# One 4 MB weight load in two halves on two queues, and two 1 KB loads moved to GpSimd

## The chip, the cores and the metric

The kernel runs on one core of a Trainium2 chip. Its time is device microseconds (us) of one execution, and what is compared is the median of several executions. A profile is one further execution, recorded instruction by instruction; its times are counted from the start of its span.

## What is computed

The kernel is one decode step of a block that mixes two branches by a gate. With one token `x` of 512 numbers:

```python
g = sigmoid((x * gate_w).sum(-1))
q = x @ wq                        # 512 x 4096: 32 heads of 128
k, v = the last 4096 rows of 8 cached heads, each shared by 4 query heads
a = softmax(q k^T / sqrt(128)) v @ wo
b = (sigmoid(x @ w_gate) * (x @ w_up)) @ w_down
out = g * a + (1 - g) * b
```

All inputs are bf16. What has to be read is 30.67 MB: `wq` and `wo` 4 MB each, the keys and the values 8 MB each, and `w_gate`, `w_up`, `w_down` 1.75 MB each. The result is 1 KB. Every weight is used once, for one row.

## The kernel before, in words

**Loads.** All large loads are issued by SyncE (SP) on one queue, in the order written in the kernel: `wq` (line 80, one DMA of 128 partitions x 32 KB), four key blocks `kn` of 2 MB (line 84, in a helper called four times), `w_gate` (94), most of `w_up` (99), the rest of `w_up` as four loads `wx` of 32 partitions (105), four value blocks `vv` (84 again), two halves of `wo` (115), and `w_down` in four pieces `wd` (120). The two 1 KB inputs `x` and `gate_w` are issued by ScalarE (ACT) on its own queue (lines 74 and 75). They land in the one-partition tile `xr`. The result leaves by ScalarE's queue too (343).

**Waits of the loads.** The framework deals the loads that SyncE and ScalarE issue over eight semaphores in turn, so a load may be issued only when the load eight places before it has landed. A `vv` load also waits until the transposes on VectorE (DVE) have read the `kn` buffer that it overwrites, and `wo` waits for the last reader of `wq_sb`.

**Start of the compute.** GpSimd (POOL) builds an identity (`identf`, `ident`), a block of ones, a zeroed `qbig` and a permutation (lines 123 to 133). TensorE (PE) turns `x` into a column `xT` by four tiny matmuls against `ident` (148), and a piece of it into `xx` (155) after VectorE has copied it to `xp` (153). VectorE multiplies `x` by `gate_w` and sums (165, 166), makes `selI` and `other` (143, 140), and copies `xT` and `xx` out of PSUM (158, 160). VectorE takes its work in exactly this order, so everything from line 165 on stands behind the landing of `gate_w`. TensorE then fills the score banks with a mask (182, it needs `other`), sums the gate (168), and starts on `q`.

**The rest.** `q` is 8 blocks of 4 matmuls (200) that need `xT` and `wq_sb`; ScalarE copies each block out (202), VectorE transposes (205) and scatters into `qbig` (216). Eight key transposes on VectorE (188) feed 64 score matmuls (227). Softmax, then 64 value matmuls (299) as the value blocks arrive, then the up projection (243, 240), `wo` and `w_down` row by row into one accumulator (290), and two copies to `res` (341, 342). The order on TensorE, VectorE and ScalarE is that of the program text from line 177 on.

Of the kernel before, what the change touches and what calls it, by code (L numbers as in the profile page):

```python
# [17 lines left out]
def kernel(  # L18
# [14 lines left out]
    nc = tc.nc  # L33

    P = 128
# [35 lines left out]


    xr = const.tile([1, 2, D], BF16, name="xr")
    nc.scalar.dma_start(xr[:, 0, :], A_x[0, :, :])
    nc.scalar.dma_start(xr[:, 1, :], gate_w.rearrange("(o n) -> o n", o=1))

    dq = nc.sync
    wq_sb = big.tile([P, DC, HQ * DH], BF16, name="wq_sb", tag="big")
    wq_v = A_wq.rearrange("(p c) n -> p c n", c=DC)
    dq.dma_start(wq_sb[:], wq_v)  # L80


    def load_pair(t, cache, a, n0=0, n1=NP):
# [290 lines left out]
```

## Time and profile before

| | us |
|---|---|
| median of 6 executions | 80.45 (80.27 to 80.68) |
| the profiled execution's own time | 80.68 |
| its span in the profile | 79.0 |
| TensorE busy | 52.4 |
| VectorE busy | 38.8 |
| ScalarE busy | 10.9 |
| GpSimd busy | 3.3 |
| DMA bytes / mean rate over the span | 30.71 MB / 389 GB/s |

The span leaves out 1.7 us of the profiled execution's own time (80.68 less 79.0), which lie before its first and after its last instruction. The profile names 16 DMA engines; its queue q1 carries SyncE's loads (2608 packets, 30.67 MB, 92.4% of the 16 engines' span), and q10 carries ScalarE's (6 packets). A "packet" is what one engine moves at a time: for `wq` a whole row of 32 KB. The trace also keeps when each engine reported the end of its share of a load ("landing"). In the timeline a suffix q (SPq, ACTq) is the sequencer of an engine issuing a DMA.

### The profile page before, as it was taken

How to read it: one execution, taken by the hardware profiler on the slowest of the kernel's cores; microseconds unless marked ns; L12 is line 12 of the kernel's file. 1: busy time of each engine (PE TensorE's matmuls, PEld its weight loads, DVE VectorE, ACT ScalarE, POOL GpSimd, SP SyncE). 2: the span in 40 equal slices, each digit the busy share in tenths (PEclk: the TensorE clock that was granted, in tenths of full speed). 3: DMA queues.
4: the chain of work that ended last, by engine and by line, in shares of the span. 5: the costliest groups of instructions: out<-in, count | busy, mean ns of one | idle time of the engine just before them, and what ended most of it. 6: DMA issues, size and time to landing. Idle time of an engine off the chain costs nothing.

```text
span 79.0 us, 798 instructions
## 1 busy us (share of the span) xinstructions
PE 52.4 (66%) x314; PEld 23.6 (30%) x314; DVE 38.8 (49%) x52; ACT 10.9 (14%) x20; POOL 3.3 (4%) x10
## 2 busy tenths in 40 slices
PE   0200182999914788998888307999996699567650
PEld 0200131344402333333332202344341345345420
DVE  1601820019959999999996339963000000690020
ACT  2400000237742000000001191000000002000010
POOL 7900000000000000000000000000000000000000
PEclk9999999999999999999999995699999999999997
DMA  6779899999999999999999999999999999999700
GB/s 183 282 332 515 381 431 390 415 440 448 423 415 464 423 415 414 436 414 428 405 466 390 423 440 440 423 415 440 431 440 398 423 440 448 398 398 398 266 17 1
DMA packets 2616, 30.71 MB, mean 389 GB/s; under 512 B 307, under 2 KB 438, under 8 KB 822
## 3 DMA queue, kind: packets, MB, share of 16 engines
q1 hardware_dynamic: 2608, 30.67, 92.4%
q8 instruction: 2, 0.03, 0.2%
q10 hardware_dynamic: 6, 0.00, 0.0%
HBM read 30.67 MB, written 0.00 MB: 388 GB/s over the span
## 4 chain that ended last, share of the span: by engine, by line
DMA 93%; SPq 2%; PE 1%; DVE 1%; issue 0%
DMA wd_sb<-in_B_w_down_dram 36%; DMA kn<-in_A_k_cache_dram 32%; DMA vv<-in_A_v_cache_dram 24%; SPq L84 2%; PE a_ps L290 1%; DVE res L341 1%; SPq L80 0%
## 5 line engine op out<-in xcount | busy, mean ns | idle before, releaser
L299 PE MATMUL pv_ps<-vv,eT 128*32 128x512 bf16 x64 | 15.8, 405 | 4.1 <-DVE eT L271 2.8
L227 PE MATMUL S_ps<-kT,qbig 128*128 128x512 bf16 x64 | 15.2, 378 | 5.0 <-DVE qbig L216 2.8
L188 DVE STREAM_TRANSPOSE kT<-kn 128x2048 f32<-128x2048 f32 x8 | 17.8, 2282 | 0.0
L227 PEld LDWEIGHTS <-qbig 128*128 128x128 bf16 x64 | 6.1, 97 | 14.1 <-issue 4.2
L299 PEld LDWEIGHTS <-eT 128*32 128x32 bf16 x64 | 6.2, 102 | 13.0 <-issue 4.2
L200 PE MATMUL q_ps<-wq_sb,xT 128*128 128x512 bf16 x32 | 8.7, 441 | 1.6 <-DMA wq_sb<-in_A_wq_dram 1.6
L318 DVE TENSOR_TENSOR oT<-o_ps,rb 128x32 bf16<-128x32 f32 x1 | 0.2, 192 | 13.6 <-PE o_ps L316 13.6
L205 DVE STREAM_TRANSPOSE qtT<-q_sb 128x512 f32<-128x512 f32 x4 | 2.7, 693 | 7.4 <-ACT q_sb L202 7.4
L182 PE MATMUL S_ps<-ident,other 2*128 2x512 bf16 x4 | 2.0, 610 | 5.6 <-DVE other L140 5.6
L202 ACT CAST q_sb<-q_ps 128x512 bf16<-128x512 f32 x8 | 4.7, 586 | 7.4 <-PE q_ps L200 7.4
L200 PEld LDWEIGHTS <-xT 128*128 128x128 bf16 x32 | 3.5, 110 | 7.3 <-issue 4.7
L290 PE MATMUL a_ps<-wo_sb,oY 128*1 128x256 bf16 x64 | 3.8, 272 | 1.5 <-DMA wo_sb<-in_A_wo_dram 1.2
L290 PEld LDWEIGHTS <-oY 128*1 128x1 bf16 x64 | 2.7, 83 | 3.1 <-issue 1.4
L271 DVE STREAM_TRANSPOSE eT<-e_sb 128x1024 bf16<-128x1024 bf16 x2 | 2.4, 1224 | 1.9 <-ACT e_sb L269 1.9
L254 ACT ACTIVATE sge<-gu_ps 128x448 f32<-128x448 f32 x1 | 0.5, 545 | 18.9 <-PE gu_ps L243 18.9
L309 ACT COPY pv_sb<-pv_ps 128x512 f32<-128x512 f32 x1 | 0.6, 586 | 17.8 <-PE pv_ps L299 17.8
L341 DVE CAST res<-a_ps 1x256 bf16<-1x256 f32 x1 | 0.4, 411 | 5.2 <-PE a_ps L290 5.2
L281 DVE RECIPROCAL sg<-sge 128x448 f32<-128x448 f32 x1 | 3.0, 2952 | 0.0
L249 DVE TENSOR_REDUCE pm<-S_ps 128x1 f32<-128x1024 f32 x2 | 2.4, 1207 | 0.9 <-PE S_ps L227 0.9
L165 DVE TENSOR_TENSOR gpr<-xr 1x512 f32<-1x512 bf16 x1 | 0.7, 678 | 4.4 <-DMA xr<-in_gate_w_dram 4.4
L290 PE MATMUL a_ps<-wd_sb,hT 128*1 128x256 bf16 x28 | 2.0, 271 | 0.8 <-DMA wd_sb<-in_B_w_down_dram 0.8
L148 PE MATMUL xt_ps<-ident,xr 1*128 1x1 bf16 x4 | 0.3, 167 | 3.5 <-POOL ident L126 3.5
(62 smaller groups left out, 31.1 us busy)
## 6 DMA issues: line engine op xcount, KB each, us to landing
kn<-in_A_k_cache_dram SPq DMA_DIRECT2D x4, 2048.0 KB, 27.5
vv<-in_A_v_cache_dram SPq DMA_DIRECT2D x4, 2048.0 KB, 19.1
wq_sb<-in_A_wq_dram SPq DMA_DIRECT2D x1, 4096.0 KB
wo_sb<-in_A_wo_dram SPq DMA_DIRECT2D x2, 2048.0 KB
wg_sb<-in_B_w_gate_dram SPq DMA_DIRECT2D x1, 1792.0 KB
wu_sb<-in_B_w_up_dram SPq DMA_DIRECT2D x1, 1456.0 KB
wd_sb<-in_B_w_down_dram SPq DMA_DIRECT2D x1, 1024.0 KB
wd_sb<-in_B_w_down_dram SPq DMA_DIRECT2D x1, 384.0 KB
```

The source lines that it names most:

```text
L84: dq.dma_start(t[:, n0:n1, :].rearrange("p n d -> p (n d)"), cache[0, 2 * a:2 * a + 2, SBASE:SBASE + W, :] .rearrange("y (x n) d -> x y n ...
L182: nc.tensor.matmul(S_ps[u // 2][:, u % 2, :], lhsT=other[:].rearrange("p o y u -> p (o y u)"), rhs=ident[0:2, 0:2].rearrange("p (o y) -> p ...
L188: nc.vector.transpose(t[:].bitcast(F32), kn[a][:, v * KB:(v + 1) * KB, :] .rearrange("p n d -> p (n d)").bitcast(F32))
L200: nc.tensor.matmul(q_ps[:], lhsT=xT[:, c:c + 1].to_broadcast([P, P]), rhs=wq_sb[:, c, ks], start=(c == 0), stop=(c == DC - 1))
L202: nc.scalar.copy(q_sb[:, ks], q_ps[:])
L205: nc.vector.transpose(qtT[:].bitcast(F32)[:, kq], q_sb[:].bitcast(F32)[:, kq])
L227: nc.tensor.matmul(S_ps[v][:, hb, :], lhsT=q_st[:, a, dhi, :, t], rhs=k_v[:, hb * 16:(hb + 1) * 16, dhi, :, t], start=False, stop=(a == HP ...
L249: nc.vector.tensor_reduce(pm2[:, v:v + 1], S_ps[v][:].rearrange("p a b -> p (a b)"), axis=AX.X, op=ALU.max)
L271: nc.vector.transpose(eT[:, :, v * KB:(v + 1) * KB, :].rearrange("p a n r -> p n a r"), e_sb[:, v, :].rearrange("p (n a r) -> p n a r", a= ...
L281: nc.vector.reciprocal(sg[:], sge[:])
L290: nc.tensor.matmul(a_ps[32 * i:32 * i + 1, i, 0:HN], lhsT=lhsT, rhs=rhs[:, i * HN:(i + 1) * HN], start=start, stop=stop)
L299: nc.tensor.matmul(pv_ps[32 * a:32 * a + 32, :, :], lhsT=eT[:, a, 4 * m:4 * m + 4, :].rearrange("p n r -> p (n r)"), rhs=vv[a][:, 4 * m:4 ...
```

## The change

`x` and `gate_w` are issued by GpSimd, ahead of its other work. `wq` becomes two DMAs of 64 partitions, the even ones issued by SyncE and the odd ones by ScalarE, each row still 32 KB; both fill the same tile, and its readers wait for both. Nothing that computes is changed, and the order of instructions on TensorE and VectorE is the same as before.

```diff
     xr = const.tile([1, 2, D], BF16, name="xr")
-    nc.scalar.dma_start(xr[:, 0, :], A_x[0, :, :])
-    nc.scalar.dma_start(xr[:, 1, :], gate_w.rearrange("(o n) -> o n", o=1))
+    nc.gpsimd.dma_start(xr[:, 0, :], A_x[0, :, :])
+    nc.gpsimd.dma_start(xr[:, 1, :], gate_w.rearrange("(o n) -> o n", o=1))
 
     dq = nc.sync
     wq_sb = big.tile([P, DC, HQ * DH], BF16, name="wq_sb", tag="big")
     wq_v = A_wq.rearrange("(p c) n -> p c n", c=DC)
-    dq.dma_start(wq_sb[:], wq_v)
+
+    for y, queue in enumerate((dq, nc.scalar)):
+        queue.dma_start(wq_sb[y:P:2], wq_v[y:P:2])
```

In the program as built, GpSimd's two loads are cut into 16 pieces of 32 numbers (64 B) each, and they have semaphores of their own. The two halves of `wq` take the first two of the eight semaphores, so `kn` begins at the third instead of the fourth, and all later loads follow: each waits for the same load as before, but for three. Line 99 waited for `x` and now waits for nothing; the first `wx` load waited for `wq` and now waits for its odd half; the second `wx` load waited for `gate_w` and now waits for the even half of `wq`.

## The prediction

> **What bounds the kernel now.** I read the strip of 40 slices first. After the first slices the 16 DMA engines are busy to the end, and TensorE is not.
>
> ```profile
> PE   0200182999914788998888307999996699567650
> DMA  6779899999999999999999999999999999999700
> GB/s 183 282 332 515 381 431 390 415 440 448 423 415 464 423 415 414 436 414 428 405 466 390 423 440 440 423 415 440 431 440 398 423 440 448 398 398 398 266 17 1
> ```
>
> The reader is to see that the rate is flat (398 to 466 GB/s) from the seventh slice to the third from last, so the only soft places are the start (183, 282, 332) and the last 4 us. Next, the chain of work that ended last, in order of time:
>
> ```profile
> 0.73 0.37 SPq L80
> ...
> 2.53 25.40 DMA kn<-in_A_k_cache_dram
> ...
> 28.01 19.11 DMA vv<-in_A_v_cache_dram
> ...
> 47.13 28.69 DMA wd_sb<-in_B_w_down_dram
> 75.83 0.04 issue
> 75.87 0.62 PE a_ps L290 x6
> 76.49 0.40 DVE res L341
> ```
>
> Loads follow each other from 0.73 to 75.83 us; compute adds about 1 us at the end. The packet records of the trace say the same more sharply: from its second or third packet on, each engine takes 1.213 us for a 32 KB row of `wq` (27.0 GB/s, 432 GB/s for 16), one row after another without a gap. So the time is: start of the first packet, plus bytes at that rate, plus the tail. The bytes do not change. Only the start, the rate of `wq`, and what is put between its rows can. Third, the start itself, from the timeline:
>
> ```profile
> 0.73 0.49 ACTq L74 DMA_DIRECT2D xr<-in_A_x_dram  x1
> ...
> 0.73 0.37 SPq L80 DMA_DIRECT2D wq_sb<-in_A_wq_dram  x1
> ...
> 1.17 2.65 SPq L84 DMA_DIRECT2D kn<-in_A_k_cache_dram  x4
> 1.26 0.21 ACTq L75 DMA_DIRECT2D xr<-in_gate_w_dram  x1
> ...
> 7.66 0.68 DVE L165 TENSOR_TENSOR gpr<-xr 1x512 f32<-1x512 bf16 x1 [4.39 <-DMA xr<-in_gate_w_dram]
> ...
> 11.56 0.10 PEld L200 LDWEIGHTS <-xT 128*128 128x128 bf16 x1 [0.84 <-issue]
> ...
> 13.28 8.73 PE L200 MATMUL q_ps<-wq_sb,xT 128*128 128x512 bf16 x32 [1.64 <-DMA wq_sb<-in_A_wq_dram]
> ```
>
> SyncE and ScalarE issue at the same moment. TensorE is ready for `q` at 11.56 us, 3.9 us after `gate_w` is there, and waits for `wq` until 13.28. Last, from the waits, what slack TensorE has behind that:
>
> ```profile
> PE pv_ps L299 <- DMA vv<-in_A_v_cache_dram: 1.3, 1, 1.3
> PE a_ps L290 <- DMA wo_sb<-in_A_wo_dram: 1.2, 1, 1.2
> PE a_ps L290 <- DMA wd_sb<-in_B_w_down_dram: 0.8, 2, 0.6
> ```
>
> Three times it has caught up with the loads: 1.3 + 1.2 + 0.8 = 3.3 us of later `q` cost nothing at the end.
>
> **The change part by part.** I work against the profiled execution's 80.68 us; it was the slowest of the six, 0.23 above the median, and I move the sum to the median at the end.
>
> *Issuing `wq`.* One issue of 374 ns goes; two are added, side by side. The issue ahead of the first packet sets the DMA start, and behind it stand `kn` on SyncE (queue full until 75.8, hidden) and the table load of 1.28 us on ScalarE (first used at 10.37, hidden). The halves step over every second row, which no load of before does; the nearest rows are `wq`'s own 374 ns, and `kn`, whose source has a step more, at 605 to 662. So the first packet moves by 0 to +0.25 us; the built program prepares `wq`, `wo` and `wd` ahead in a way that it does not do for `kn`, `vv`, `wx` and the halves (`wd`'s issues take 328 to 430 ns, `vv`'s 535 to 581), so I take +0.2.
>
> *Two queues fill 16 engines.* The 16 first packets of `wq` began between 1.73 and 2.88 us, a spread of 1.15 us. If two queues with half the rows each halve it, the last engine starts 0.58 us sooner; if not, nothing. The end is set by the latest engines of sixteen, not by an average one, but I cannot tell whether those are the late starters. Take -0.15, bounds -0.58 and 0.
>
> *The rate of `wq`.* Before, 128 rows go to 16 engines, 8 rows each: 8 x 1.213 = 9.7 us. After, each half is 64 rows, and with 16 engines 4 + 4 rows are the same 9.7 us. That is one bound, 0. The other comes from `wx`, the one load under 128 partitions: in the trace each of its four loads has landings of 8 engines, `wq` of 16. If 64 rows run at half the engines, or two engines get in each other's way, `wq` takes 19.4 us and everything behind it is 9.7 us later. Nearest row: `kn`, whose source steps over 64 places of two rows, and which runs on 16 engines at 611 ns per 16 KB, full rate. I take 0 and keep +9.7 as an end.
>
> Which partitions a load reaches is what the Trainium skill speaks about here: "SBUF — State Buffer", section "Door 1: The DMA port swizzle", says that DMA rate depends on how many of 16 ports the partitions reach, and that 64 partitions from 0 reach 8; even partitions reach all 16, but only if the engines do not meet on one port at the same time, which the page does not say for this shape. Two engines a port would be an estimated 218 GB/s for `wq`, 19.2 us by that page instead of 9.7. "DMA: Bandwidth & Descriptors", section "Rules for kernel authors", speaks against the change as a whole: spreading loads over issuing engines, or over two sets of partitions, brings no bandwidth. By that rule the sum has no gain but in the start. No row of before has two large loads on two queues.
>
> *`x` and `gate_w` on GpSimd.* Two issues of 493 and 209 ns leave ScalarE and stand ahead of all of GpSimd's work. No GpSimd issue is in the trace: between 0.2 us (ScalarE's shorter one) and 1.9 us (GpSimd's longest row, the memset of `qbig`) each; I take 0.5, nearest to the 0.49 of the first issue. `ident`, done at 3.42 us, slips to 4.4, at most 7.2; `selI` and `other` on VectorE stand behind `gate_w` anyway, so `gate_w` covers this.
>
> Landing: `x` was ahead of `wq` on its engine and landed at 1.96 us; `gate_w`, issued at 1.26 behind `wq`'s first rows, landed at 7.64, 6.4 us later. Now both come in 16 pieces, which need all engines and meet `wq` on each. With `gate_w`'s 6.4 us both are there by 1.7 + 6.4 = 8.1 us. VectorE then does `xp` first (1.3 us, formerly done while it waited), and TensorE is ready for `q` at 8.1 + 1.3 + 3.9 = 13.3: level with `wq`, cost 0. If two queues put twice the rows ahead (4.6 us from issue to first byte become 9.2), they land at 12.7, `q` starts at 17.9, 4.6 later than before, of which 3.3 are absorbed: +1.3 at the end.
>
> *Between the rows.* Each engine gets two pieces of 64 B and their completions; `x`'s and `gate_w`'s packets took 44 and 46 ns, completions 9: 2 x (46 + 9) = 0.11 us. Take +0.1.
>
> *`wq` done later.* If ScalarE's half falls behind, up to 4 rows of `kn` (0.61 us each) go ahead: `q` starts 2.4 us later, within the 3.3. The `vv` loads wait for VectorE's transposes, but land 19 us after issue, some 14 of them in the queue. Cost 0; without that cover, up to 2.4.
>
> Sum: +0.2 - 0.15 + 0 + 0 + 0.1 = +0.15, so 80.83 for the profiled execution and **80.6** from the median.
>
> **The rivals.**
> 1. *Half rate for `wq`* (slower). One mechanism: 64-row loads in steps of two run on 8 engines, or in pairs that share a way into SBUF, and the place is `wq`, 1.7 to 13 us. For it: `wx`'s 8 landings. Against it: `kn` at full rate. It decides from the first row on, since nothing hides a DMA that is late. Price 9.7 us, 4.9 if only half of the rows collide: 85.3 to 90.2, likeliest 90.2.
> 2. *A faster start* (faster). Two queues take 0.58 us from the spread and the issue costs nothing: 80.45 - 0.58 + 0.1 = 80.0. For it: the rate of 183 to 332 GB/s in the first three slices. Against it: the first packets took 1.7 to 2.2 us instead of 1.2, and two queues do not obviously change that.
> 3. *`x` late* (slower), as worked out: 80.6 + 1.3 = 81.9, deciding once both small loads land after 11.4 us.
> 4. *It does not do what it says*: ScalarE's half waits its turn behind SyncE's. The sum of bytes is the same: 80.5, within the forecast.
>
> **How the numbers follow.** A difference under 0.2% (0.16 us) cannot be told from none here. Forecast with rival 4: 0.45, spread over faster 0.08, same 0.20, slower 0.17, since +0.15 lies at the edge; its own range is 80.3 to 80.9. Rival 1: 0.28, slower. Rival 2: 0.17, faster. Rival 3: 0.10, slower. Together faster 0.25, same 0.20, slower 0.55. The range has to reach rival 1: 80.0 to 90.2.
>
> **What would show it.** In the profile after, the chain should again be loads from start to end. Rate of `wq`: first slices at 400 GB/s or more from the fourth on, and `q` starting at 13 to 16 us; about 216 GB/s until 20 us and packets of 2.4 us mean rival 1. Start: first packets at 1.9 us; a spread well under 1.15 us with the end of the loads before 75.5 means rival 2. The landing of `gate_w`, seen as VectorE's start on line 165, near 9.4 us; after 12.7 it is rival 3, if TensorE no longer waits for `vv`, `wo` and `wd`. The forecast is wrong if the loads end more than 0.5 us from 76.

## The result and the profile after

The median of the changed kernel is 81.05 us over 20 executions (80.82 to 82.51), against 80.55 us (80.27 to 82.01, 46 executions) for the kernel before. The ratio is **1.0065, 95% interval 1.0051 to 1.0079**: 0.52 us slower (0.0065 x 80.5). The ratios in this text, and the differences worked out from them, leave out executions that were disturbed; these occur with every kernel, before's too, and raise the plain medians a little.

The profiled execution of the changed kernel took 80.99 us, its span is 79.3. The strips of its page, which answer to the three of before:

```profile
PE   0000020199999327898888893059999999697650
DMA  0999897999999999999999999999999999999700
GB/s 0 281 513 430 364 529 323 422 447 413 438 422 446 430 422 422 426 434 421 406 444 433 397 422 455 422 422 413 463 413 422 422 438 430 426 389 394 282 23 1
```

The first slice is empty (before: 183 GB/s), the third is at 513. `wq` runs at the full rate, but it begins later. TensorE is empty for five slices, and full from the ninth slice on.

The chain of work that ended last, in order of time (start, duration, what):

```profile
1.23 0.51 POOL xr L74
...
1.85 11.91 DMA xr<-in_gate_w_dram
...
13.78 0.69 DVE gpr L167
...
17.76 8.66 PE q_ps L202 x32
...
38.00 6.67 DVE kT L190 x3
...
44.68 0.54 SPq L86
...
47.32 28.63 DMA wd_sb<-in_B_w_down_dram
75.95 0.04 issue
76.00 0.66 PE a_ps L292 x6
76.65 0.40 DVE res L343
```

This chain has a new middle. Before, it went from load to load; now it goes through the late `gate_w`, `q` and the key transposes to an issue of SyncE, and then to `wd`. One must not read 11.91 us of loss in it. The step at 44.68 is a `vv` load that waited for a transpose, and while it waited the DMA strip stayed at 9: there was other work in the queue. The chain says who released whom, not that the DMA engines stood still.

The start, from the timeline (start, duration, engine, line, tile; in brackets the idle time before and who ended it):

```profile
0.73 0.56 SPq L82 DMA_DIRECT2D wq_sb<-in_A_wq_dram  x1
0.74 0.55 ACTq L82 DMA_DIRECT2D wq_sb<-in_A_wq_dram  x1
...
1.23 0.62 POOL L74 DMA_DIRECT2D xr<-in_A_x_dram  x1 [0.79 <-POOLq L360]
...
1.85 0.48 POOL L75 DMA_DIRECT2D xr<-in_gate_w_dram  x1
...
10.86 0.33 DVE L155 COPY xp<-xr 1x64 bf16<-1x64 bf16 x2 [9.67 <-DMA xr<-in_A_x_dram]
...
13.78 0.68 DVE L167 TENSOR_TENSOR gpr<-xr 1x512 f32<-1x512 bf16 x1 [2.59 <-DMA xr<-in_gate_w_dram]
...
17.69 6.55 PE L202 MATMUL q_ps<-wq_sb,xT 128*128 128x512 bf16 x22
```

The two halves are issued side by side, each in 0.55 us instead of 0.37. `x` is there at 10.8 us instead of 2.0, `gate_w` at 13.8 instead of 7.6, and `q` starts at 17.69 instead of 13.28. And what TensorE still waits for behind that:

```profile
PE a_ps L292 <- DMA wd_sb<-in_B_w_down_dram: 0.8, 2, 0.6
...
PE a_ps L292 <- DMA wo_sb<-in_A_wo_dram: 0.4, 1, 0.4
```

The wait for `vv` is gone, that for `wo` fell from 1.2 to 0.4, that for `wd` is as it was. TensorE has caught up once more before the end, so 4.4 us of later `q` did not reach it in this execution.

Where the 0.5 us are, then, is read from a few stations. The table holds them for three executions: before on record, a second profile of the same kernel taken later (80.36 us, nearer to its usual time), and after. "Tail" is the execution's own time less the landing of the 256 KB piece of `wd`, the last load that compute waits for.

| us | before, on record | before, second profile | after |
|---|---|---|---|
| first packet of `wq` begins | 1.73 | 1.74 | 2.10 |
| the 16 first packets begin until | 2.88 | 2.53 | 2.72 |
| the 16 first packets end | 3.52 to 4.40 | 3.50 to 4.34 | 3.90 to 4.41 |
| `wq` landed | 13.23 | 13.17 | 13.56 |
| 256 KB of `wd` landed | 75.82 | 75.47 | 75.95 |
| tail | 4.86 | 4.89 | 5.04 |
| own time | 80.68 | 80.36 | 80.99 |

Against the second profile: 0.63 = 0.48 of loads that end later + 0.15 of tail. Against the profile on record the loads would have lost only 0.13; that execution was the slowest of its six, and a comparison with it alone misses most of the loss.

Single stations scatter, and one pair of profiles settles little. Seven profiles of kernels that load `wq` with one DMA of 128 rows (both of before, e1, e7, e8, e9 and e11 below) have their first packet at 1.73 to 1.76 us and the 256 KB of `wd` at 75.44 to 75.83. After, e3 and e4, with halves, have 2.07 to 2.10 and 75.77 to 75.98. The first packets are clear of each other; the ends of the loads overlap.

### The profile page after: what moved, and what is told of

Read it like the earlier page. It is cut to its first block, busy times and chain, and to the rows that moved or that the text cites. A ratio compares the mean times of both kernels' runs of the same rounds, so it can differ in the third digit from the quotient of the medians.

```text
span 79.3 us, 800 instructions
## 1 busy us (share of the span) xinstructions
PE 50.4 (64%) x314; PEld 23.0 (29%) x314; DVE 37.9 (48%) x52; ACT 10.9 (14%) x20; POOL 4.4 (6%) x12
## 4 chain that ended last, share of the span: by engine, by line
DMA 51%; DVE 19%; PE 14%; issue 7%; SPq 3%; ACT 1%; POOL 1%; DVEq 0%; POOLq 0%
DMA wd_sb<-in_B_w_down_dram 36%; DMA xr<-in_gate_w_dram 15%; DVE kT L190 14%; PE q_ps L202 11%; PE S_ps L184 2%; DVE qbig L218 2%; SPq L117 1%; SPq L122 1%; DVE qtT L207 1%; DVE gpr L167 1%; DVE gsum L168 1%; PE a_ps L292 1%; ACT q_sb L204 1%; SPq L86 1%; POOL xr L74 1%
## 5 line engine op out<-in xcount | busy, mean ns | idle before, releaser
L301 PE MATMUL pv_ps<-vv,eT 128*32 128x512 bf16 x64 | 13.8, 405 | 2.8 <-DVE eT L273 2.8
L301 PEld LDWEIGHTS <-eT 128*32 128x32 bf16 x64 | 5.7, 102 | 10.0 <-DVE eT L273 2.9
```

Source lines behind the costliest of these rows:

```text
L301: nc.tensor.matmul(pv_ps[32 * a:32 * a + 32, :, :], lhsT=eT[:, a, 4 * m:4 * m + 4, :].rearrange("p n r -> p (n r)"), rhs=vv[a][:, 4 * m:4 ...
```

## The experiments

There were four ideas. **S** (start): the issue of a load that steps over every second row takes longer, and all packets follow later (e6 shows that the step is not what makes the issue long). **T** (tail): the result's issue on ScalarE takes longer. **L** (late): the small loads come late, and through `q` part of it reaches the end. **G**: a GpSimd load in the program costs time at the kernel's end.

### e1_small_on_gpsimd: `x` and `gate_w` alone

```diff
-    nc.scalar.dma_start(xr[:, 0, :], A_x[0, :, :])
-    nc.scalar.dma_start(xr[:, 1, :], gate_w.rearrange("(o n) -> o n", o=1))
+    nc.gpsimd.dma_start(xr[:, 0, :], A_x[0, :, :])
+    nc.gpsimd.dma_start(xr[:, 1, :], gate_w.rearrange("(o n) -> o n", o=1))
```

> Only x and gate_w move to GpSimd; wq stays one load of 128 rows from SyncE. Theory S (the start: a half with a row step issues in 0.56 us instead of 0.37, and the first packet comes 0.37 us later): nothing left of the loss, 80.5, first packet at 1.73. Theory T (the tail: with x and gate_w gone from ScalarE, its last DMA, the result, pays a first-use issue of 0.48 us instead of 0.22): 80.75, the result's issue at 0.48 us. Rival L (late gate_w moves q, and q moves the end): gate_w lands later than 7.6 us and the time rises by as much as PE then has no wait left for wd.

Measured: ratio 1.0036 (1.0026 to 1.0047), +0.29 us. The profiled execution took 80.65. First packet at 1.75 and `wd` landed at 75.54, as before; `x` landed at 8.17, `gate_w` at 10.61, `q` began at 14.54. Tail 5.11, the longest of all. So S is not the whole: with an unchanged start, about 0.29 us are lost, and most of them are in the tail (0.22 more than in the second profile of before). The number fitted T, but e4 shows that T's mechanism is not the cause.

### e2_halves_only: the two halves of `wq` alone

```diff
-    dq.dma_start(wq_sb[:], wq_v)
+    for y, queue in enumerate((dq, nc.scalar)):
+        queue.dma_start(wq_sb[y:P:2], wq_v[y:P:2])
```

> Only wq is split, even rows from SyncE, odd rows from ScalarE; x and gate_w stay on ScalarE ahead of the odd half. Theory S: 80.8 to 80.9, first packet at 2.1, result issued in 0.22 us. Theory T: 80.5, result issued in 0.22 us. Rival L: 80.5, since x lands by 2 us again; gate_w before 8.

Measured: ratio 1.0052 (1.0036 to 1.0067), +0.42 us; issues of 562 and 504 ns, first packet at 2.08. The profiled execution took 82.43 us, so only its start is read here. ScalarE's half is issued behind `x` and `gate_w` here, at 1.51 us.

### e3_halves_sp: both halves on SyncE

```diff
-    for y, queue in enumerate((dq, nc.scalar)):
+    for y, queue in enumerate((dq, dq)):
```

(against e2). One queue again, but the halves and their row step stay.

> wq is split by even and odd rows, but both halves are issued by SyncE, one after the other; x and gate_w stay on ScalarE. This is the row step without a second queue. Theory S: 80.8 to 81.0, first packet at 2.1, and with one queue the first packets of the 16 engines spread as widely as before (1.1 us) instead of 0.6. Theory T: 80.5. Rival L: 80.5.

Measured: ratio 1.0051 (1.0033 to 1.0069), +0.41 us, the same as e2. First packet at 2.07, `wd` landed at 75.77. From this kernel's timeline, both issues in one line:

```profile
0.73 1.19 SPq L82 DMA_DIRECT2D wq_sb<-in_A_wq_dram  x2
```

Two issues take 1.19 us, 564 and 571 ns each by the line's own statistics; the second queue is not needed for it. `q` starts at 13.22 here, as early as before, and 0.41 us are lost all the same: L has no part in it. Shown is that the halves alone make the first packet 0.33 us later and cost 0.41 us, on one queue as on two. That the late first packet is what arrives at the end is argued from the two sizes: `wd`'s 75.77 lies within what kernels without halves show. The spread of the first packets is 0.70 us here on one queue and 0.62 after, against 1.15 in before's profile on record; but it is 0.78 in before's second profile and 0.89 in e4, whose `wq` is loaded as in the changed kernel, so nothing can be read from it.

### e4_warm_out: a ScalarE load in the middle

```diff
+    warm = const.tile([1, D], BF16, name="warm")
+    nc.scalar.dma_start(warm[:], A_x[0, :, :])
```

(in the changed kernel, in the middle of the run; nobody reads the tile.) T held that ScalarE's issue of the result is slow when it is the engine's first small one since the start.

> The changed kernel with one DMA more: ScalarE loads 1 KB into a tile that nobody reads, in its idle time after the copy of line 311 (about 65 us), so that the result is no longer its first DMA of that shape. Theory T: 0.26 us faster than the changed kernel, 80.75, result issued in 0.22 us. Theory S: 81.0, as the changed kernel. Rival L: 81.0.

Measured: ratio 1.0081 (1.0039 to 1.0123); the eight executions with a granted TensorE clock (the mean share of full speed that TensorE had, as the profile reports it) of 0.957 or more took 80.77 to 81.00 us, the profiled one 80.93. Three at 0.936 took 81.49 to 81.98 and make the interval wide (e8 comes back to them; why they are late stays open). The result's issue, from the timeline of the changed kernel and then of this one:

```profile
77.13 0.48 ACTq L345 DMA_DIRECT2D out_dram<-res  x1
```

```profile
77.16 0.23 ACTq L347 DMA_DIRECT2D out_dram<-res  x1
```

The issue is 0.25 us shorter and the end does not move: from the beginning of the issue the result needs 1.11 us to land where the issue is long, 1.09 us where it is short. **T falls.** What the write waits for runs beside the issue.

### b1_before: a second profile of the kernel before

> The kernel before, unchanged, for a second profile. The profile on record was the slowest of its six executions, and its slowest first row of wq ended at 4.40 us, 0.3 later than the next. If that is what its 0.2 us above the median are, this profile has its slowest first row done by 4.1 to 4.2 us, and the wd load of two rows (wd2) landed by 75.5 to 75.6 instead of 75.82. If not, 4.40 and 75.8 again.

Measured: 80.36 us, `wd` landed at 75.47 as expected. But the 16 first packets ended at up to 4.34 us, as in the profile on record, so the first row isn't what made that execution longer. It stays open what did; the traces show where: the first `kn` block landed 0.07 us later than here (27.93 and 27.86), the first `vv` block 0.37 (47.12 and 46.75), and `wd` 0.35.

### e5_cols: halves by columns, 128 rows each

```diff
-        queue.dma_start(wq_sb[y:P:2], wq_v[y:P:2])
+        queue.dma_start(wq_sb[:, 2 * y:2 * y + 2, :], wq_v[:, 2 * y:2 * y + 2, :])
```

(in the changed kernel.) Two queues, but no row step; rows of 16 KB.

> The changed kernel, but wq is halved by columns of every row: 128 rows of 16 KB from SyncE, 128 from ScalarE. Two queues as in the change, and no step over rows. Theory S (the row step's longer issue is the start cost): issue 0.37 us, first packet at 1.73, and of the change's +0.52 only the GpSimd part is left: 80.75. If two queues in themselves are the start cost: first packet at 2.1 and 81.0. If two queues gain once the issue is short: under 80.6.

The issues, from the statistics of line 82 of this kernel (duration in ns, smallest/median/largest):

```profile
L82 ACTq DMA_DIRECT2D wq_sb<-in_A_wq_dram x1: 401/401/401, 0.7 to 0.7; - x1
L82 SPq DMA_DIRECT2D wq_sb<-in_A_wq_dram x1: 377/377/377, 0.7 to 0.7; - x1
```

377 and 401 ns, and the first packet at 1.74 us: with 128 rows in each load the start is that of before again. Ratio 1.0056 (1.0027 to 1.0086), wide because of one execution of 81.90; the median of the ten executions that it counts is 80.77, 0.2 below the changed kernel's 80.97. That is S's direction, though the interval alone would not show it. `wd` landed at 75.70.

### e6_blocks: partitions 0 to 63 and 64 to 127

```diff
-        queue.dma_start(wq_sb[y:P:2], wq_v[y:P:2])
+        queue.dma_start(wq_sb[64 * y:64 * y + 64], wq_v[64 * y:64 * y + 64])
```

> The changed kernel, but wq is halved into partitions 0 to 63 and 64 to 127 instead of even and odd. If engines can get in each other's way on the way into SBUF, as rival 1 had it, this is where they should: wq at about half rate, packets near 2.4 us, and up to 9.7 us more than the change: 86 to 91. If 16 engines write any 64 rows at full rate: 81.0, as the change, packets 1.21 us.

Measured: ratio **1.1256 (1.1224 to 1.1287)**, +10.1 us; the two executions behind it took 90.51 and 90.64, the profiled one 92.14. The strips of its page (a slice is 2.26 us here):

```profile
DMA  4889999995999999999999999999999999999400
GB/s 101 203 174 217 232 232 232 232 232 123 406 428 435 435 406 435 435 406 431 431 420 398 465 406 428 428 420 435 428 435 420 435 420 428 428 395 382 168 19 0
```

The DMA strip says 9 and the rate says 232: the engines are busy and move half; the busy strip alone would not have told. The packet records say it row by row: a 32 KB row takes 2.3 to 2.6 us in most cases (median 2.40) instead of 1.213, and `wq` lands at 23.35 instead of 13.56. The 16 engines are in the same half most of the time: at 9 us all 16 in SyncE's, at 11 us all 16 in ScalarE's. With even and odd rows they are often in one half together as well (at 6 us all in SyncE's, at 7 us all in ScalarE's), and most rows take 1.213 us.

The Trainium skill, "SBUF — State Buffer", section "Door 1: The DMA port swizzle", says that partitions 0 to 63 reach half of the ports; by its table of ports the even partitions reach all of them. Its figure of about 218 GB/s for half the ports stands beside 232 measured, and the full rate of the even and odd rows agrees with the table.

The same run corrects S. These halves step over no row, and yet their issues are as long as those of the change, and the first packet comes at 2.08 us:

```profile
L82 SPq DMA_DIRECT2D wq_sb<-in_A_wq_dram x1: 577/577/577, 0.7 to 0.7; - x1
L82 ACTq DMA_DIRECT2D wq_sb<-in_A_wq_dram x1: 541/541/541, 0.7 to 0.7; - x1
```

So the long issue and the late first packet go with a `wq` load of 64 rows, stepped (after, e2, e3, e4) or not (e6); with 128 rows, in one load or two (before, e1, e5, e10), both are short. Why 64 rows are prepared more slowly is open.

### e7_pool_dma: one idle GpSimd load

```diff
+    idle = const.tile([1, D], BF16, name="idle")
+    nc.gpsimd.dma_start(idle[:], A_x[0, :, :])
```

(in the kernel before, behind GpSimd's other work; nobody reads the tile.)

> The kernel before with one DMA more: GpSimd loads 1 KB into a tile that nobody reads, after it has made ident (about 3.4 us), with all other loads, their order and their waits as before. Theory G (a GpSimd DMA in the program costs at the end of the kernel whatever it is for: GpSimd's clearing of semaphores 0.14 us instead of 0.10, its drains, and some 0.06 outside the span): +0.13, 80.65. If the cost of the small loads on GpSimd is instead that they land late and move q: 80.5, no difference.

Measured: ratio 1.0019 (1.0006 to 1.0031), +0.15 us. **G holds** as a cost; where it arises is open. What the records of the last two microseconds show: with a GpSimd load in the program, GpSimd's clearing of the semaphores takes 142 ns instead of 96, and two of its last drain instructions 93 and 40 ns instead of 78 and 34; those are 0.07 us (in the changed kernel 139, 98 and 40). But the recorded span is no longer for it: from the result's landing to the last instruction, one of VectorE's, it is 0.97 us here as in both profiles of before (0.98 and 0.97).

The same records hold a second cost, of another kind. SyncE closes by waiting for all semaphores, two an instruction, in a fixed order, each 0.06 us or so. The result's landing ends one of these waits; what stands behind it is paid in full. After the landing come 1 wait before, 2 after, 3 in e1, 2 in e2, e3, e5 and e10, and 1 in e4 and e7. From the landing to the last instruction it is 0.97 to 0.99 us with one, 1.03 to 1.08 with two, and 1.11 with three. The change has moved the result's write to another semaphore.

### e8_late_q and e11_late_q2: `q` 3.5 us later, nothing else

```diff
-    for u in range(4):
+    for w in range(16):
+        u = w % 4
...
-                         start=True, stop=False)
+                         start=True, stop=(w < 12))
```

(in the kernel before: the four mask matmuls of line 182 are done four times, with the same values, so that `q` begins at 16.74 us.)

> The kernel before, but the four mask matmuls of line 182 are done four times over (12 more on TensorE, same values), so that q starts at about 17.4 us instead of 13.28, as it does in the changed kernel (17.69), with every load as before. Theory S+G (the change's loss is made at the start of the loads and at the end of the kernel; the late gate_w is absorbed): 80.5, and TensorE's wait for vv gone. Rival L (late q is part of the loss): 80.7 or more.

Measured: ratio 1.0031 (0.9999 to 1.0062). The profiled execution took 80.30 us with `wd` landed at 75.44, as before; of the three waits that made up the slack one is left, from the waits of this kernel:

```profile
PE a_ps L291 <- DMA wd_sb<-in_B_w_down_dram: 0.7, 2, 0.5
```

But two of eight executions took 81.3. They had a mean granted TensorE clock of 0.936. So the kernel was run again:

> The same kernel as the one with 16 mask matmuls (q at 16.74 us, repeated mask matmuls that write the same values), run again, to see whether its scatter goes with the granted TensorE clock. In the eight executions of the first time, those with a mean clock of 0.957 or more took 80.30 to 80.66 us, those with 0.935 to 0.936 took 80.66, 81.30 and 81.33; the kernel before took 80.42 to 80.69 at 0.935. If the remaining slack of TensorE is thin and a lower clock uses it up: executions at 0.95 or more within 0.2 us of the kernel before, those at 0.936 later by 0.3 to 0.9 us, and the kernel before itself no later at 0.936. If the scatter has another cause: late executions at both clocks, or early ones at 0.936.

Measured: ratio 1.0012 (0.9986 to 1.0038). Both runs together, by granted clock: 11 executions at 0.957 or more took 80.27 to 80.66, median 80.46 (the kernel before: 80.47, 48 executions at 0.95 or more). Seven at 0.935 to 0.936 took 80.26, 80.53, 80.66, 80.97, 81.19, 81.30 and 81.33 (before: 80.36 to 80.69, 12 executions). All late ones are at the lower clock, but not all at the lower clock are late. So at the higher clock a `q` that is 3.5 us later costs nothing, and the slack that is left may be thin enough for a lower clock to use it up. The mean clock alone doesn't decide. In the traces TensorE has half its clock in stretches of 3.4 us: three of them in b1, whose mean is 0.935 (from 24.7, 48.6 and 69.0 us), two in e8's profile at 0.957 (from 28.5 and 52.4). No late execution was profiled, so whether the place of a stretch decides is open. Among the executions of the changed kernel that its ratio counts there is one such, 81.63 at 0.936.

### e9_later_q: `q` 8.65 us later

The same edit with 28 mask matmuls.

> The same with the mask matmuls done seven times over: q at about 23.1 us, 9.8 later than before. This asks where the slack ends. By the prediction's 3.3 us of slack: +6.5, 87.0. By what is left of TensorE's waits in the changed kernel (0.4 for wo and 0.8 for wd at a delay of 4.4, so 5.6 in all): +4.2, 84.7.

Measured: ratio 1.0356 (1.0316 to 1.0396). In its profile (83.71 us) `q` begins at 21.93 and the last matmul ends at 79.48 instead of 76.1: 8.65 us later at the start are 3.4 later at the end (76.1 is the end in before's second profile), so **5.3 us** were absorbed, not 3.3. By the ratio, +2.9 us from three executions, it would be 5.8. The end of its chain:

```profile
56.99 5.14 PE pv_ps L300 x16
...
62.47 8.11 PE pv_ps L300 x45
...
74.29 5.23 PE a_ps L291 x92
79.52 0.40 DVE res L342
```

There is no load left in it: TensorE is the bound. Where the further 2 us of slack were is seen in the value matmuls. Their statistics, of before and of after ("first and last start"):

```profile
L299 PE MATMUL pv_ps<-vv,eT x64: 376/379/634, 48.0 to 65.1; 128*32 128x512 bf16 x64
```

```profile
L301 PE MATMUL pv_ps<-vv,eT x64: 379/379/634, 52.4 to 66.1; 128*32 128x512 bf16 x64
```

The same 64 matmuls take 17.1 us before and 13.7 after (and 13.9 in e9). Only 1.3 of the 3.4 us stood in the list of waits, as one wait for `vv`. The rest is not a slower pace: at full clock a matmul starts 216 ns after the one before it in both kernels. The timelines, two lines of before and one of after:

```profile
53.27 7.30 PE L299 MATMUL pv_ps<-vv,eT 128*32 128x512 bf16 x32
61.87 2.97 PE L299 MATMUL pv_ps<-vv,eT 128*32 128x512 bf16 x13 [1.30 <-DMA vv<-in_A_v_cache_dram]
```

```profile
57.64 8.19 PE L301 MATMUL pv_ps<-vv,eT 128*32 128x512 bf16 x45
```

In the last line 45 matmuls take 8.19 us, under 216 ns each. Each matmul of the group fills 32 of 128 columns, and each value block has its own 32. Where the next block is there already, its first four matmuls start 5 to 17 ns after the last four of the block before, side by side with them. That happens at two places after and in e9, at one in before's second profile (whose group takes 16.2 us), at none in before's profile on record. So the 3.4 us are 1.5 and 0.2 of later starts at the fourth and the third block, and 8 x 0.216 = 1.7 of matmuls that could not run side by side. No list of waits holds these 1.7. With `wo` and `wd`, 3.4 + 1.2 + 0.8 = 5.4 us, close to the slack that e9 measured.

### e10_cols_act: columns on two queues, small loads on ScalarE

```diff
-    dq.dma_start(wq_sb[:], wq_v)
+    for y, queue in enumerate((dq, nc.scalar)):
+        queue.dma_start(wq_sb[:, 2 * y:2 * y + 2, :], wq_v[:, 2 * y:2 * y + 2, :])
```

(in the kernel before: two queues without a row step and without GpSimd.)

> wq halved by columns (128 rows of 16 KB on each of SyncE and ScalarE), and x and gate_w on ScalarE ahead of its half: two queues, short issue, no GpSimd DMA. If the loss is the row step's issue plus the GpSimd DMA and nothing else, little is left: 80.5 to 80.6, first packet at 1.73. If two queues or the 16 KB pieces cost something themselves: 80.7. If two queues gain: under 80.4, and this would be the best of all.

Measured: ratio 1.0038 (1.0016 to 1.006). First packet at 1.74, `wd` landed at 75.44 in the profiled execution, which took 80.44. No gain from two queues; by its ratio this is nearest to the 80.7 of "two queues or the 16 KB pieces cost something themselves". `q` waits until 16.33 us here, since ScalarE's half, issued at 1.52, lands at 16.29. Of the nine executions that the ratio counts, six had a clock of 0.914 and took 80.64 to 81.18; the other three took 80.44, 80.52 and 80.68. That looks like e8, but no run of before at that clock stands beside it, so it is argued only.

### The terms together

Three terms: the start (0.33 to 0.36 with halves of 64 rows, the first packet's shift), a GpSimd load (0.15, from e7), and 0.06 for each closing wait above one.

| | start | GpSimd | closing | sum | measured, with 95% |
|---|---|---|---|---|---|
| after | 0.36 | 0.15 | 0.06 | 0.57 | 0.52 (0.41 to 0.64) |
| e1 | - | 0.15 | 0.12 | 0.27 | 0.29 (0.21 to 0.38) |
| e2 | 0.34 | - | 0.06 | 0.40 | 0.42 (0.29 to 0.54) |
| e3 | 0.33 | - | 0.06 | 0.39 | 0.41 (0.27 to 0.56) |
| e4 | 0.34 | 0.15 | - | 0.49 | 0.65 (0.31 to 0.99) |
| e5 | - | 0.15 | 0.06 | 0.21 | 0.45 (0.22 to 0.69) |
| e10 | - | - | 0.06 | 0.06 | 0.31 (0.13 to 0.48) |

For after, e1, e2, e3 and e4 the sum lies within the interval. For e5 and e10 it lies below: both hold single executions well above the rest, but that the two column loads, which only these kernels have, cost about 0.25 us by themselves is not excluded. The 0.36 is the shift of the first packet and the 0.06 the length of a wait, both read from traces; no run varied either alone.

## Why the prediction was right and where it was wrong

The bound was right: loads from start to end. So was the direction that it held likeliest, slower. The size was not: 80.6 forecast, and 80.45 + 0.52 = 80.97 measured on its footing, just outside the 80.3 to 80.9 that it gave this case; only the wide range, stretched to 90.2 for the first rival, holds it. The sum said +0.15 and the chip +0.52. By its steps:

- **Issuing `wq`, +0.2.** Mis-sized: +0.36. The issue did grow by the forecast 0.19 us (564 ns less 374). But the first packet comes 0.80 us after the issue's end instead of 0.62, and the prediction had counted the issue alone. e3 shows the whole shift on one queue. The reason given, the step over every second row, was wrong: e6 has issues of 577 and 541 ns without a step. That +0.19 came out even so is luck.
- **Two queues fill 16 engines, -0.15.** Nothing. The spread went from 1.15 to 0.62 us, and the prediction would have read that as its gain. But it took one profile's 1.15 for a property of the kernel: the unchanged kernel's second profile has 0.78. And what fell was no gain: the first packets end at 4.41 at the latest, 4.40 before. e2 and e3 differ by 0.01 us, so the second queue gives nothing. "DMA: Bandwidth & Descriptors", section "Rules for kernel authors", said that spreading loads over issuing engines brings no bandwidth, and the runs agree.
- **The rate of `wq`, 0.** Right: 1.213 us for most rows, SyncE's and ScalarE's in turn.
- **`x` and `gate_w` on GpSimd.** The issues took 617 and 484 ns, near the 0.5 chosen. The landing failed: 13.76 us for `gate_w` instead of 8.1. The far bound, 12.7, was nearer, for a reason that the prediction didn't have: an engine takes one GpSimd descriptor, then one row from each other queue, 2.43 us for two rows. `x`'s data came at 7.55, its semaphore a turn later at 9.97, `gate_w`'s data a turn later again. With one queue of rows (e1) `x` landed at 8.17 and `gate_w` at 10.61.
- **What that costs, 0.** Right, but by a cover that was larger than counted. `q` began 4.4 us later; against the 3.3 of the prediction this would have cost 1.1. Slack was read from the waits alone, which leave out the matmuls that could not run side by side while their block was missing: 5.3 to 5.8 by e9.
- **Between the rows, +0.1.** Smaller: each engine had four such packets of 11 ns, 0.04 us.
- **`wq` done later, 0.** Right; it landed 0.4 later, and the start had done that.
- **Missing.** The end of the kernel had no term: 0.15 for a GpSimd load in the program (e7) and 0.06 for one more closing wait.
- **The strip.** It was read a little too smooth: from the seventh slice to the fourth from last the rate is 390 to 466 GB/s, and the third from last is at 266. Nothing in the sum hangs on it.

The rivals: *half rate* is real and 10.1 us dear, but for 64 adjacent partitions (e6), not for every second one. The price worked out for it, 9.7, was right, and the doubt that made it 0.28 likely was about the wrong pairing of partitions. *A faster start* did not come. *`x` late* had its landing (13.76, over 11.4) and its `q` (17.69, forecast 17.9), and the price of 1.3 us did not follow. *It does not do what it says* is excluded: from the second row on, rows of both queues alternate.

## What to carry to other kernels

When one queue already keeps all DMA engines busy, a second one gives nothing, and what is left to lose is at the edges: the preparation of the first load and the closing of the kernel. To measure slack behind a stall, compare how long a group of instructions takes with and without its data at hand; the listed waits leave out what could have run side by side. Before a station or a spread of one profile is read as an effect, look at it in a second profile of the same kernel. If a load must be split over partitions, compare rates and not busy strips: interleaved halves ran at full rate here, adjacent ones at half.

## What the runs showed of the hardware that was not expected

- A small GpSimd load takes turns with the rows of other queues, and its completion takes a turn of its own. 1 KB took 9.6 and 11.9 us from issue to landing beside two queues of 32 KB rows.
- The issue of a `wq` load of 64 rows takes 0.50 to 0.58 us, with a row step or without, one of 128 rows 0.36 to 0.40; where it is the first load, its first packet comes 0.13 to 0.18 us later still.
- The two copies on line 153 got six times faster by being late. From the statistics of before, then of after:

```profile
L153 DVE COPY xp<-xr x2: 1155/1204/1254, 2.0 to 2.1; 1x64 bf16<-1x64 bf16 x2
```

```profile
L155 DVE COPY xp<-xr x2: 197/202/207, 10.9 to 11.0; 1x64 bf16<-1x64 bf16 x2
```

Before, GpSimd was at its 1.86 us memset of `qbig` at that time; after, it had finished at 5.5 us. 64 elements cost 1.2 us beside GpSimd and 0.2 us alone. The prediction had counted 1.3 us for them in its path to `q`. That they waited for GpSimd is argued from the times; no run moved the memset alone.
